# Attention and a ResMLP block on one core: another order of the first transposes, and one row turned by transfer

## The chip, the cores and the metric

One core of a Trainium2 chip runs the whole program. The metric is device microseconds of one execution, the median over runs. The engines named below: PE (TensorE, matrix products and transposes into PSUM), DVE (VectorE), ACT (ScalarE), POOL (GpSimd), SP (SyncE, which here only issues transfers). Transfers are issued from the queues of SP, POOL and ACT.

## The reference

Attention with 16 query heads and 4 key heads over 8 batches of 384 tokens, head size 64, and behind it a ResMLP block with width 1024 and 4096 hidden units:

```python
q, k, v: (8, 16, 384, 64), (8, 4, 384, 64), (8, 4, 384, 64)   # each k, v head serves 4 q heads
attn = softmax(q @ k.T / 8)                                    # per head
x = (attn @ v) as (8, 384, 1024)
a1 = alpha1 * x + beta1
tok = einsum('ts,bsd->btd', w_tok, a1)
u = x + lam * tok
a2 = alpha2 * u + beta2
out = u + lam * (relu(a2 @ w_ch1) @ w_ch2)
```

All inputs and the output are f32; the kernel computes its products in bf16.

## The kernel before

**Stages.** The kernel handles the batches in passes. Pass 0 and pass 1 multiply batches 0 and 1 by w_ch1 and w_ch2 (`main`). Passes 2, 3 and 4 take two batches each, (2, 3), (4, 5), (6, 7), and use a scheme of seven products instead of eight (`pair`). Such a scheme needs sums and differences of the blocks of its operands beforehand: `sums_a` builds them of the activations, `sum_w1` and `sum_w2` of the weights. The attention and the token mixing of the batches to come (`side`) are woven into the second product of the pass before: batch 0 stands alone at the start, batch 1 lies beside pass 0, batches 2 and 3 beside pass 1, 4 and 5 beside pass 2, 6 and 7 beside pass 3.

**The order is written out by hand.** Each engine executes its instructions in the order in which the program emits them. `main` and `pair` yield after every four matmuls or so; at each such place the program emits what `plan` holds for that place. For the second batch of a pair the places are those of its table plus 38 (`put_all(ps, 1, side(c + 1)[1], lambda u: u + 38)`).

**A side.** A batch's 16 heads are eight pairs p = 0 to 7, which are also eight rows of 128 columns of the 1024. `scores(i)` multiplies turned q and turned k (L279) into a PSUM tile of two banks, and ACT takes the exponential of 1024 columns at a time (L288). `av(p)` multiplies by v (L315), DVE divides (L320, L323) and scales (L328, L330). `tok_flip(p)` mixes the tokens (L340), adds (L347), scales to bf16 (L351), writes u out with a transfer from SP (`spill`, L243), and turns the row: a2 of row p must stand with its columns on the partitions before w_ch1 can use it. There are two ways to turn it:

- `a2_transpose(p)`, a transposing transfer from SP (L362), issued right behind the spill;
- `turn(p)`, three transposes on PE into a PSUM bank (L428) and one copy by ACT (L430), at a place of their own some steps later.

`by_pe(p)` chooses: for batch 1 row 7 is turned on PE; for batches 3, 5, 7 rows 5, 6, 7.

**Banks of a side beside a pair.** `three()` gives the three PSUM tiles sc0, sc1, sc2 out in turn, by the counter `pairs["turn"]`; while `pairs["held"]` is set, one of them belongs to the product and is passed over. Scores, av, tok and turn all take theirs from it. Beside pass 1 the three tiles come from a pool that rotates by itself.

**The hand-over.** For batches 4 to 7 `sums_a(0, 2)` stands at place 76, `sums_a(2, 1)` at 79 and `sums_a(3, 1)` at 81 of the pass before. Call (j, n) forms three sums (L587, L588, L589) from rows j to j + n - 1 and 4 + j to 4 + j + n - 1 of both batches; (0, 2) therefore reads rows 0, 1, 4 and 5. For batches 2 and 3 there are four calls at places 41, 42, 45 and 47, the second of which reads rows 1 and 5. In the next pass the first matmuls (X, L723, o = 1) read unmixed rows of the even batch; the ones behind them (Y, o = 7) read what L588 wrote, one row per matmul, rows j = 0 to 3 in order. Row 7 of batch 3 is written to the same buffer as its row 5 (two buffers, tag a2).

**The start.** Transfers bring k's heads 0 and 1 (SP, L150), the first two and the next two heads of q (ACT, L879), the other q groups, v and w_tok (POOL), and short rows of alpha, beta and lam (SP, L869). DVE and ACT cast k to bf16 twice side by side (`place_k`, L160). k is turned in bf16 on PE and copied by DVE (`k_transpose`, L255, L257); the first two pairs of q are turned in f32 straight from their staging area (`q_transpose`, L265) and copied by ACT (pair 0) or DVE (pair 1) (L267). `warmup(n)` emits n matmuls of 384 columns whose results nobody reads (L844): nine at the very start, three behind the first scores, one behind the fourth. `scale_rows` and `split` (L903, L911, L913) prepare the short rows on DVE; the first needs lam. The list `us` of `side(0)` is emitted front to back, and `load_k(1)` is emitted behind its fourth entry.

Of the kernel before, what the change touches and what calls it, by code (L numbers as in the profile page):

```python
# [12 lines left out]
def kernel(  # L13
# [40 lines left out]
    NP = Hq // 2  # L54
    D1 = D + 1
    NPL = 2
# [14 lines left out]
    threes, pairs = [], {}  # L71
# [23 lines left out]
    turn, a2_turn = [0], [0]  # L95
# [45 lines left out]
    def load_k(b, hs=(0, 2)):  # L141
        if b > 1:
            k_tile(b)
            for a in range(2):
                nc.gpsimd.dma_start(out=k2s[b][:, :, a], in_=by_head(k[b]))
            return
        for h in hs:
            ks[b, h // 2] = t = hTf[:, 7680 + 384 * h:8448 + 384 * h].bitcast(f32).rearrange(
                "p (h st d) -> p h st d", h=2, st=NST)
            nc.sync.dma_start(out=t, in_=by_head(k[b, h:h + 2]))  # L150
# [40 lines left out]
    def bank(shape, tag, name, dtype=f32):  # L191
        if tag == "mm":
            return mms.tile(shape, dtype, tag="mm", name=name, bufs=2)
        return psum.tile(shape, dtype, tag=tag, name=name, bufs=2 if tag == "sc" else 1)

    def three():
        if pairs:
            pairs["turn"] = (pairs["turn"] + 1 + (pairs["turn"] == 2 and pairs["held"])) % 3
            return pairs["sc%d" % pairs["turn"]].tile([P, 2, 4, P], f32, tag="sc", name="sc", bufs=1)
        return threes[0].tile([P, 2, 4, P], f32, tag="sc", name="sc", bufs=3)  # L200

    def one():
        return three()[:, 0]
# [25 lines left out]
    def side(b):  # L229
# [41 lines left out]
        def scores(i, later=False):  # L271
            sc = bank([P, 2, 4, P], "sc", "sc") if first else three()
            k = 4 * i
            while k < 4 * i + 4:
                n = min(4 * i + 4, k - k % NST + NST) - k
                p, sk, st = k // (NST * NST), k // NST % NST, k % NST
                for hh in range(2):
                    r = slice(hh * D, (hh + 1) * D)
                    nc.tensor.matmul(out=sc[:, hh, k % 4:k % 4 + n], lhsT=kT[r, 2 * p // G, BLK[hh][sk], :],  # L279
                                     rhs=qT[r, p, st:st + n, :], start=True, stop=True)  # L280
                k += n

            def exp():
                if first:
                    e = hTf[:, i % 6 * 1024:(i % 6 + 1) * 1024].rearrange("p (h k s) -> p h k s", h=2, k=4)
                else:
                    e = sb.tile([P, 2, 4, P], bf, tag="es", name="es", bufs=EB)
                nc.scalar.activation(out=e, in_=sc, func=EXP, scale=scale_qk)  # L288
                ess[i] = e
                exps[0] = 0 if first else 2  # L290

            if later:
                late.append(exp)
            else:
                exp()
# [40 lines left out]
        def tok(p):  # L336
            ps = bank([P, NST, P], "mm", "tok") if first else three()[:, 0, :NST]
            for tt in range(NST):
                for st in range(NST):
                    nc.tensor.matmul(out=ps[:, tt, :], lhsT=wtokT[:, st, tt * P:(tt + 1) * P],  # L340
                                     rhs=a1s[p][:, st, :], start=(st == 0),
                                     stop=(st == NST - 1 and not first))
                if first:
                    nc.tensor.matmul(out=ps[:, tt, :], lhsT=R[:, tt * P:(tt + 1) * P],
                                     rhs=H[:, cols(p)], start=False, stop=True)
            u = x_of(p)
            nc.vector.tensor_tensor(out=u, in0=ps, in1=u, op=ADD)  # L347
            if first:
                return
            a2s[p] = next_a2() if b > NPL + 1 else sb.tile([P, NST, P], bf, tag="a2", name="a2", bufs=2)  # L350
            nc.vector.tensor_tensor(out=a2s[p], in0=u, in1=bc(al2, p), op=MUL)  # L351
# [50 lines left out]
        def add(f, *a):  # L402
            us.append(lambda: f(*a))
# [12 lines left out]
        def flip(p):  # L416
            if not first:
                spill(p)
            if not by_pe(p):
                a2_transpose(p)  # L420

        def by_pe(p):
            return b % 2 and p >= (NP - 3 if b > NPL else NP - 1)

        def turn(p):
            ps = three()[:, 0].rearrange("p a b -> p (a b)").bitcast(bf)[:, :S].rearrange("p (a b) -> p a b", a=NST)
# [5 lines left out]
        if not first:  # L432


            turns = {}
            if b == 1:
                turns = {5: [(to_all, 3, 0, 0), (load_row_set, 1, 1, 0)], 7: [(to_all, 3, 1, 1), (load_row_set, 2, 0, 1)],
                         9: [(k_transpose, 0)], 12: [(to_all, 1, 0, 2)], 14: [(to_all, 1, 1, 0), (load_row_set, 2, 1, 0)],
                         17: [(scale_beta,)], 20: [(to_all, 2, 0, 1)], 22: [(to_all, 2, 1, 0)],
                         24: [(q_transpose, 0, 2, "av")], 28: [(k_transpose, 2)]}  # L440
                for i in range(3):
                    turns[32 + 4 * i] = [(q_transpose, 2 + 2 * i, 2, "av")]
            if (b - NPL) // 2 > 0:
                at = {}

                def put(k, *m):
                    at.setdefault(k, []).append(m)

                for j in range(6):
                    put((0, 6, 12, 21, 26, 31)[j], scores3, j, j in (2, 5))  # L450
                for p in range(NP):
                    put((4, 10, 14, 18, 24, 29, 33, 35)[p], av, p)
                    put((8, 15, 17, 22, 27, 32, 36, 38 if b % 2 else 39)[p], tok_flip, p)
                    if by_pe(p):
                        put((36, 39, 41)[p - NP + 3], turn, p)
                return turns, at
            return turns, {
                0: [(scores3, 0)], 4: [(av, 0)], 6: [(scores3, 1)], 8: [(tok_flip, 0)], 11: [(av, 1)],
                13: [(scores3, 2, True)], 15: [(av, 2)], 16: [(tok_flip, 1)], 18: [(tok_flip, 2)], 19: [(av, 3)],
                21: [(scores3, 3)], 23: [(tok_flip, 3)], 25: [(av, 4)], 27: [(scores3, 4)], 29: [(tok_flip, 4)],  # L460
                31: [(av, 5)], 33: [(scores3, 5, True)], 35: [(av, 6), (tok_flip, 5)], 37: [(av, 7)],
                38: [(tok_flip, 6)], 41: [(tok_flip, 7)],
                **{39 + 4 * i - i // 2 * 2: [(turn, p)] for i, p in enumerate((5, 6, 7)) if by_pe(p)}}
        add(k_transpose, 0, 1)
        add(q_transpose, 0, 1, "av", "ACT")
        add(place_k, 0, 0, (1,))
        add(q_transpose, 1, 1, "tp")
        lower, upper = range(NP // 2), range(NP // 2, NP)
        ut = a2_transpose
        at = {0: [(warmup, 3), (scale_rows, 0), (split, 0, 1, 0)], 1: [(k_transpose, 1, 1)],  # L470
              2: [(q_transpose, 2, 2, "av"), (split, 0, 1, 1)], 3: [(warmup, 1)],
              4: [(av, 0)], 5: [(spread, lower, "tp"), (a1, 0)], 6: [(av, 1), (k_transpose, 2, 2, "tp")],
              7: [(q_transpose, 4, 2, "av"), (a1, 1)], 8: [(av, 2)],
# [365 lines left out]
    with tc.manual_schedule(engines=order):  # L839

        def warmup(n):
            warm = bank([P, 512], "mm", "warm")
            for _ in range(n):
                nc.tensor.matmul(out=warm[:, :S], lhsT=wtokT[:, 0, :P], rhs=wtokT[:, 1, :],  # L844
                                 start=True, stop=True)

        nc.vector.memset(wtokT, 0.0)
        warmup(9)
        load_k(0, [0])

        rows_f = hTf[:32, 9216:10496].bitcast(f32)
# [107 lines left out]
        for i, f in enumerate(side(0)):  # L959
            f()  # L960
            if i == 3:
                load_k(1)
# [8 lines left out]
        def put(ps, phase, at, *m):  # L971
            plan.setdefault((ps, phase, at), []).append(m)
# [6 lines left out]
        def put_flips(ps, phase, b, places):  # L979
            for u, m in zip(places, ((flip_k, b), *((flip_q, b, i, 2) for i in range(0, NP, 2)))):  # L980
                put(ps, phase, u, *m)

        turns, at = side(1)
        put_all(0, 0, turns)
        put_all(0, 1, at)
        put_flips(0, 1, 2, (34, 36, 37, 42, 43))

        put(0, 1, 45, load_next, 3)
        put_all(1, 0, side(2)[1], lambda u: int(1.5 * u))
        put_flips(1, 0, 3, (53, 55, 57, 59, 61))  # L990
        put_all(1, 1, side(3)[1])
# [68 lines left out]
```

## Time and profile before

| | us |
|---|---|
| median of 3 runs | 740.01 (739.26 to 740.1) |
| the profiled execution, its own time | 739.53 |
| its span in the profile | 737.7 |
| PE busy in the span | 731.3 |
| DVE busy | 515.4 |
| ACT busy | 325.2 |
| mean granted PE clock | 0.999 of full |

The span runs from the first instruction of the program to the end of the last; the execution's own time has 1.83 us around it. All durations of single instructions below come from that one execution. A line of the timeline gives start, length, engine, line of the code, operation and tiles; several instructions of one kind in a row are merged (x3), and the length is then that of the group. Matmul records overlap, since the next one starts before the last one has drained; what a matmul costs PE is the distance from start to start.

What the transfers that turn rows look like, and who turned rows on PE (all instructions that write or read the tile `ops`):

```profile
L362 SPq DMA_TRANSPOSE ops<-obuf x26: 1238/1288/2234, 326.9 to 570.0; - x26
L362 SPq DMA_TRANSPOSE ops<-a x20: 1240/1296/3387, 87.0 to 225.0; - x20
L430 ACT COPY ops<-sc x10: 479/480/480, 129.0 to 585.4; 128x384 bf16<-128x384 bf16 x10
DMA to landing us min/median/max: 2.4/5.0/9.8
```

The first two lines are issues (ns: shortest, median, longest), and the last is the time from issue to landing for those of them that the view could match.

### The profile page before, as it was taken

How to read it: one execution, taken by the hardware profiler on the slowest of the kernel's cores; microseconds unless marked ns; L12 is line 12 of the kernel's file. 1: busy time of each engine (PE TensorE's matmuls, PEld its weight loads, DVE VectorE, ACT ScalarE, POOL GpSimd, SP SyncE). 2: the span in 40 equal slices, each digit the busy share in tenths (PEclk: the TensorE clock that was granted, in tenths of full speed). 3: DMA queues.
4: the chain of work that ended last, by engine and by line, in shares of the span. 5: the costliest groups of instructions: out<-in, count | busy, mean ns of one | idle time of the engine just before them, and what ended most of it. 6: DMA issues, size and time to landing. Idle time of an engine off the chain costs nothing.

```text
span 737.7 us, 14512 instructions
## 1 busy us (share of the span) xinstructions
PE 731.3 (99%) x5769; PEld 418.9 (57%) x5769; DVE 515.4 (70%) x993; ACT 325.2 (44%) x469; POOL 164.0 (22%) x211
## 2 busy tenths in 40 slices
PE   8999999999999999999999999999999999999998
PEld 5866555566555566655555566555555566654444
DVE  7773366457587889749777987847968988762354
ACT  7632431455332566653334366664343266660000
POOL 9434221420000232211012244020002222000011
PEclk9999999999999999999999999999999999999999
DMA  9999999999999999999979999998989999937965
GB/s 187 194 201 200 207 216 174 176 187 208 217 271 257 179 221 212 260 269 201 296 186 219 181 145 192 207 246 199 269 242 152 223 136 143 173 115 262 288 189 103
DMA packets 218017, 151.32 MB, mean 205 GB/s; under 512 B 88660, under 2 KB 197060, under 8 KB 217948
## 3 DMA queue, kind: packets, MB, share of 16 engines
q0 software_dynamic: 120304, 64.60, 67.0%
q1 hardware_dynamic: 96956, 85.33, 42.7%
q8 instruction: 45, 0.74, 0.4%
q10 hardware_dynamic: 688, 0.46, 0.2%
q14 instruction: 24, 0.20, 0.1%
HBM read 154.84 MB, written 38.27 MB: 262 GB/s over the span
## 4 chain that ended last, share of the span: by engine, by line
PE 93%; DVE 3%; DMA 3%; SPq 1%; issue 0%; ACT 0%; DVEq 0%
PE C L789 30%; PE X L723 17%; PE h L532 10%; PE ch L570 9%; PE Y L723 8%; PE sc L279 4%; PE Z L723 4%; PE sc L315 4%; PE sc L340 3%; DMA ops<-a 2%; PE h L223 1%; DMA hT<-in_moe_lam_dram 1%; PE tok L340 1%; SPq L176 0%; PE av L315 0%; DVE xr L323 0%
## 5 line engine op out<-in xcount | busy, mean ns | idle before, releaser
L288 ACT ACTIVATE es<-sc 128x1024 bf16<-128x1024 f32 x126 | 121.4, 1023 | 155.9 <-PE sc L279 144.8
L789 PE MATMUL C<-w,arena 128*128 128x512 bf16 (+2 forms) x744 | 168.3, 372 | 0.0
L789 PEld LDWEIGHTS <-arena 128*128 128x128 bf16 x1040 | 94.8, 98 | 100.5 <-issue 5.1
L728 ACT ACTIVATE hT<-X,bias 128x384 f32<-128x384 f32 x144 | 83.7, 582 | 61.8 <-PE X L723 54.8
L723 PEld LDWEIGHTS <-w 128*128 128x128 bf16 x768 | 75.1, 98 | 50.1 <-issue 0.2
L517 POOL DMA_DIRECT2D out_dram<-hT x33 | 28.8, 871 | 283.5 <-DVE hT L688 106.1
L570 PE MATMUL ch<-arena,hT 128*128 128x512 bf16 x384 | 90.8, 379 | 0.0
L185 POOL DMA_DIRECT2D w<-in_moe_w_ch_dram x68 | 62.8, 965 | 98.2 <-PE X L723 34.2
L532 PE MATMUL h<-ops,w 128*128 128x384 bf16 (+1 forms) x480 | 83.3, 327 | 0.3
L723 PEld LDWEIGHTS <-pad 128*128 128x128 bf16 x576 | 56.4, 98 | 37.2
L723 PE MATMUL X<-ops,w 128*128 128x384 bf16 x384 | 70.2, 326 | 0.0
L723 PE MATMUL X<-ops,pad 128*128 128x384 bf16 x384 | 70.2, 326 | 0.0
L789 PE MATMUL C<-pad,arena 128*128 128x512 bf16 (+2 forms) x296 | 70.2, 373 | 0.0
L532 PEld LDWEIGHTS <-w 128*128 128x128 bf16 x480 | 45.4, 98 | 29.8 <-issue 2.1
L570 PEld LDWEIGHTS <-hT 128*128 128x128 bf16 x384 | 34.7, 98 | 36.8 <-issue 2.5
L347 DVE TENSOR_TENSOR xr<-sc,xr 128x384 f32<-128x384 f32 x56 | 31.0, 553 | 24.3 <-PE sc L340 24.3
L315 PEld LDWEIGHTS <-es 128*128 128x128 bf16 x1008 | 38.3, 97 | 12.4
L340 PEld LDWEIGHTS <-wtokT 128*128 128x128 bf16 x576 | 37.5, 98 | 11.8 <-DVE a L330 0.8
L279 PE MATMUL sc<-qT,kT 64*128 64x384 bf16 (+2 forms) x576 | 41.8, 271 | 0.7 <-DVE xr L323 0.3
L320 DVE RECIPROCAL rinv<-sc 128x6 f32<-128x6 f32 x56 | 10.8, 192 | 44.3 <-PE sc L315 44.1
L315 PE MATMUL sc<-v,es 128*128 128x65 bf16 x1008 | 39.9, 193 | 0.0
L723 PE MATMUL Z<-ops,w 128*128 128x384 bf16 x192 | 39.0, 326 | 0.0
(138 smaller groups left out, 910.3 us busy)
## 6 DMA issues: line engine op xcount, KB each, us to landing
w<-in_moe_w_ch_dram POOLq DMA_DIRECT2D x68, 512.0 KB, 10.7
w<-w2s SPq DMA_DIRECT2D x60, 512.0 KB, 4.6
pad<-w2s SPq DMA_DIRECT2D x24, 512.0 KB, 7.2
out_dram<-xr SPq DMA_DIRECT2D x56, 192.0 KB, 6.1
out_dram<-hT POOLq DMA_DIRECT2D x33, 256.0 KB, 6.0
arena<-in_moe_w_ch_dram POOLq DMA_DIRECT2D x16, 512.0 KB, 20.0
w2s<-arena SPq DMA_DIRECT2D x28, 256.0 KB, 4.9
q_raw<-in_q_dram POOLq DMA_DIRECT2D x28, 192.0 KB, 10.6
```

The lines of the kernel that those rows point to most:

```text
L185: nc.gpsimd.dma_start(out=w1[:, w1_slots[c]], in_=w1src[:, :, c * CW * P:(c + 1) * CW * P])
L279: nc.tensor.matmul(out=sc[:, hh, k % 4:k % 4 + n], lhsT=kT[r, 2 * p // G, BLK[hh][sk], :], rhs=qT[r, p, st:st + n, :], start=True, stop=True)
L288: nc.scalar.activation(out=e, in_=sc, func=EXP, scale=scale_qk)
L315: nc.tensor.matmul(out=av[:, hh, sq, :], lhsT=ess[k // 4][:, m % 2, k % 4, :], rhs=vb[:, sk, hk, :], start=(sk == 0), stop=(sk == NST - 1))
L340: nc.tensor.matmul(out=ps[:, tt, :], lhsT=wtokT[:, st, tt * P:(tt + 1) * P], rhs=a1s[p][:, st, :], start=(st == 0), stop=(st == NST - 1 an ...
L347: nc.vector.tensor_tensor(out=u, in0=ps, in1=u, op=ADD)
L517: nc.gpsimd.dma_start(out=at, in_=o, accum_op=ADD)
L532: nc.tensor.matmul(out=ps[:, :n], lhsT=w1[:, w1_slots[c], dt, j * P:(j + 1) * P], rhs=a2T[:, dt, :n], start=(dt == 0), stop=(dt == NDT - 1))
L570: nc.tensor.matmul(out=ps, lhsT=hT[:, nt, ms * P:(ms + 1) * P], rhs=w2[:, row(nt)[0], row(nt)[1], cs], start=(i == 0), stop=(i == NNT - 1))
L723: nc.tensor.matmul(out=ps, lhsT=tb[g, o][:, dt, e * P:(e + 1) * P], rhs=opb(LEFT1[o])[:, dt], start=(o in (1, 2, 7) and dt == 0), stop=(dt ...
L728: nc.scalar.activation(out=snap[o, e], in_=ps, func=IDENT, bias=hi if o == 5 else lo)
L789: nc.tensor.matmul(out=x, lhsT=hid[:, t, LEFT2[o], ms * P:(ms + 1) * P], rhs=rhs[:, t % 4 * 512 + c0:t % 4 * 512 + c1], start=((not last o ...
```

## The change

Two things are changed.

**At the start** the first pair of q is turned in front of k instead of behind it, and the second pair of q is turned behind the first scores (as the first entry of that place) instead of in front of them. The idle matmuls in front are six instead of nine, and behind the first scores two instead of three.

**For the odd batches of the pairs** (3, 5 and 7) `by_pe` now takes rows 6 and 7 only. Row 5 goes the way of rows 0 to 4: a transposing transfer behind its spill. Where its `turn` stood beside a pair (place 36), the new `next_bank` moves the counter of the three tiles on by one and nothing else, so that every later user gets the tile that it had. Batch 3 has no such step.

```diff
+    def next_bank():
+        pairs["turn"] = (pairs["turn"] + 1 + (pairs["turn"] == 2 and pairs["held"])) % 3
+
     def three():
         if pairs:
-            pairs["turn"] = (pairs["turn"] + 1 + (pairs["turn"] == 2 and pairs["held"])) % 3
+            next_bank()
...
         def by_pe(p):
-            return b % 2 and p >= (NP - 3 if b > NPL else NP - 1)
+            return b % 2 and p >= (NP - 2 if b > NPL else NP - 1)
...
                     if by_pe(p):
                         put((36, 39, 41)[p - NP + 3], turn, p)
+                    elif b % 2 and p == NP - 3:
+                        put(36, next_bank)
...
+        add(q_transpose, 0, 1, "av", "ACT")
         add(k_transpose, 0, 1)
-        add(q_transpose, 0, 1, "av", "ACT")
         add(place_k, 0, 0, (1,))
-        add(q_transpose, 1, 1, "tp")
...
-        at = {0: [(warmup, 3), (scale_rows, 0), (split, 0, 1, 0)], 1: [(k_transpose, 1, 1)],
+        at = {0: [(q_transpose, 1, 1, "tp"), (warmup, 2), (scale_rows, 0), (split, 0, 1, 0)], 1: [(k_transpose, 1, 1)],
...
-        warmup(9)
+        warmup(6)
```

## The prediction

> **What bounds the kernel now.** I read the page first: busy shares, then the chain that ended last.
>
> ```profile
> span 737.7 us, 14512 instructions
> PE 731.3 (99%) x5769; PEld 418.9 (57%) x5769; DVE 515.4 (70%) x993; ACT 325.2 (44%) x469; POOL 164.0 (22%) x211
> PE 93%; DVE 3%; DMA 3%; SPq 1%; issue 0%; ACT 0%; DVEq 0%
> ```
>
> TensorE is busy 99% of the span and is 93% of the chain, so time taken off TensorE is time gained, unless another wait takes its place. The DVE and DMA shares sit in a few places. Both parts of the change touch one: the first 16 us, and the hand-over from the second matrix product of a pair to the next pair.
>
> The chain in order of time (start, length), over the first 45 us:
>
> ```profile
> 2.16 5.32 DMA hT<-in_moe_lam_dram
> ...
> 7.58 0.29 DVE hT L903
> 7.89 0.54 DVE hT L911
> 8.46 0.48 DVE hT L913
> 8.93 0.27 DVE kT L257
> 9.20 0.47 DVE qT L267
> ...
> 15.46 0.27 DVE wtokT L372
> ```
>
> Until 15.7 us the end is set neither by TensorE nor by the exponentials on ACT. The small transfer of lam lands at 7.48; DVE waits for it at L903 and then works in its order, with gaps of under 0.06 us, until the last copy of w_tok at 15.7. From there the chain is TensorE.
>
> The timeline shows the first scores, and what their order costs:
>
> ```profile
> 1.52 3.06 PE L844 MATMUL warm<-wtokT 128*128 128x384 bf16 x9 [1.52 <-DVE wtokT L847]
> 3.97 0.54 DVE L160 CAST k<-hT 128x192 bf16<-128x192 f32 x1 [0.34 <-DMA hT<-in_k_dram]
> 4.57 0.50 PE L255 MATMUL tp<-ident,k 128*128 128x128 bf16 x3
> 4.86 1.42 PE L265 MATMUL tp<-hT,arena 128*128 128x128 f32 x6
> 6.28 0.39 PE L279 MATMUL sc<-qT,kT 64*128 64x384 bf16 x4
> 6.60 0.66 PE L844 MATMUL warm<-wtokT 128*128 128x384 bf16 x3
> ```
>
> Nine idle matmuls start every 0.32 us, later ones of the same shape every 0.17: the clock records rise from half to full at 6.01.
>
> **The change, start.** k's cast ends at 4.51. The first q transfer, issued at 0.73, should land near 4.27: the second was issued at 1.25 and landed at 4.78, 3.53 later. Six idle matmuls end at 1.52 + 6 x 0.32 = 3.44, so TensorE waits 0.85 us and turns the first pair of q from 4.3 to 4.96 (3 x 0.213, the spacing of the f32 ones at 5.07 and 5.29). Then k: three at 0.107, done near 5.5, its copy on DVE (0.36) near 5.87. First scores: 5.9 instead of 6.28, 0.38 earlier. The second pair of q (0.3 to 0.6) comes behind them. ACT's first exponential gains some 0.3; the second, whose scores now wait behind q's transposes, 0.2.
>
> What is this worth at 15.7? DVE stood idle 0.70 us before L903 and the lam transfer is issued as before, second on SP behind alpha; nothing ahead of it moves. So the DVE chain starts at 7.58 again. The second pair's copy of q is then ready near 6.7 and done by 7.3: hidden in that same idle time, which is its cover; without the cover each 0.1 us of it would be 0.1 of the end. Value taken: **0**. Bounds: -0.38 (all that the scores gain) to +0.7 (clock, below). Moving load_k(1) in the program leaves it on SP behind the casts of k's other head, at 6.5 before and 6.4 after.
>
> **The change, row 5 of batches 3, 5 and 7.** Removed on TensorE: three transposes per batch (L428). Their records are 0.33 long, but what counts is start to start:
>
> ```profile
> 579.33 0.33 PE L428 MATMUL sc<-ident,obuf 128*128 128x128 bf16 x3
> 579.50 0.67 PE L340 MATMUL sc<-a,wtokT 128*128 128x128 bf16 x9
> ```
>
> 0.17 us, at full clock and with no wait: 3 x 0.17 = **-0.51 us**. ACT's three copies of 0.48 (L430) go too; ACT is idle 2.47 before them, worth nothing. The bank's turn is skipped by a counter: no cost. In batch 3 the rotation of the three banks does shift by one, but each following user gets a bank freed earlier, so nothing.
>
> Added on SP: one transposing transfer per batch, behind the spill of row 5. Issues take 1.24 to 3.39 us. In batches 5 and 7 SP has nothing else until the next spill at 582.18 (L243, issue 575.56): free. In batch 3 it pushes copies of w2 by about 1 us; they have no reader on the chain.
>
> What counts is when the row lands, for a new wait: sums_a(0, 2) on DVE (L587 to L589) reads rows 0, 1, 4, 5. Behind it DVE has the sums of rows 2 and 3, sum_w1 and L826, and the new pair's first Y product reads row 3's difference:
>
> ```profile
> 575.56 8.82 SPq L243 DMA_DIRECT2D out_dram<-xr  x3
> ...
> 584.33 0.55 DVE L587 TENSOR_TENSOR ops<-ops 128x768 bf16<-128x768 bf16 x1
> ...
> 588.62 1.46 PE L723 MATMUL X<-ops,w 128*128 128x384 bf16 x8
> 589.57 0.36 DVE L588 TENSOR_TENSOR ops<-ops 128x384 bf16<-128x384 bf16 x1
> 589.92 0.81 PE L723 MATMUL Y<-ops,w 128*128 128x384 bf16 x4
> ```
>
> DVE is busy 12.62 of the 13 us from 575 to 588, so a wait at 584.33 goes through unabsorbed. Row 3's difference ends at 589.93; the fourth Y matmul reads it at 589.92 + 3 x 0.163 = 590.41. Less 0.04 for the signal the slack is 0.44, and 0.27 once TensorE arrives 0.17 sooner.
>
> When does it land? Not by the page's median of 4.6 us, but by neighbours in the same stage, from the trace's semaphores: issued at 390.43, 396.66, 563.75, 569.98 they took 9.83, 6.75, 10.08, 8.47. Better, each lands shortly behind its spill: 0.4 to 0.6 us (five pairs), 1.9 (one), or 2.6 to 2.8 where POOL's weight loads are moving (two). Row 5's spills landed at 408.32 and 584.15, and DVE needs the row at 411.02 and 584.33.
> - Batch 5: 408.7 to 411.1. At most 0.13 late, inside the slack: 0.
> - Batch 7: 584.6 to 586.95. Late by 0.4 to 2.7 with the signal, less 0.27: a stall of 0.1 to 2.4. POOL's queue moves some 390 packets/us from 584 on, which speaks for the upper half, but the first two microseconds after the spill may be shared evenly; I take the middle, **+1.25**.
> - Batch 3: lands 2.8 to 6.0 after 232.5 by its five neighbours, so by 238.5. Its buffer is wanted by row 7 at 237.40 and its sum at 238.80; DVE has 1.58 idle before L577 at 242.32: 0.
>
> The Trainium skill ("VectorE: DVE Perf Modes", The three transpose paths) gives 1309 ns for a 128x128 turn by transfer against 390 ns on TensorE, and advises TensorE where PSUM will do. By that price, as an estimate, three blocks take 3.9 us, the row would be there at 580, and the sum would be -0.51. The trace differs: no transfer of this kind in that stage took under 6.7 once the weight loads had begun.
>
> Sum: 0 - 0.51 + 1.25 = **+0.74**: span 737.7 to 738.4. The profiled execution took 739.53, 1.83 outside its span, and is 0.48 under the median of the runs shown, so 740.01 + 0.74 = **740.75**. This kernel's runs can tell about 0.2%, 1.5 us.
>
> **Rivals.**
> *Row 5 is late in both pairs (slower).* One mechanism: its packets queue with the weight loads that POOL issues at 402.02 and 575.34, just before. It decides from the moment the row lands over 0.27 us behind DVE's arrival. For it: between the two pairs the same spill differs by 2.5 us against DVE's arrival (2.70 ahead of it, 0.18 ahead), so batch 5 can fall where batch 7 is. Against: it did not in this execution. At 2.2 per pair: 4.4 - 0.51 = +3.9, 743.9; with batch 7 alone at its upper end +1.7 to +1.9, 741.8.
> *Row 5 in time everywhere.* Stalls nought: -0.51, 739.5. For it: five pairs of eight land 0.6 or less behind their spill. Against: batch 7's spill itself lands 0.18 before the need.
> *The clock rises a step later.* The records give full clock at 6.01 and half again at 736.47, 730.45 = 214 x 3.413 apart, so decisions seem to fall on a grid of 3.41. TensorE was busy through the stretch 2.60 to 6.01 and only from 1.52 in the one before, which did not raise it. After the change 2.60 to 6.01 holds holes of 0.85 and 0.4. If that is too little, half clock lasts to 9.4: first scores 5.9 to 6.4, q 7.1, two idle ones 7.7, second scores 8.25, k 8.6, third scores 9.1, q(2,3) done 9.8, and its copy on DVE at 9.8 where it was 9.13: **+0.7**, alone with the -0.51 740.2, with the forecast's stall 741.4. For it: the one stretch that raised it was busy throughout; against: 63% busy may do.
> The Trainium skill ("TensorE: Matmul & The Clock Gate", Part 1 and Part 4) says that the gate watches a free-running window of 3413 ns and that transposes do not count as busy in the same way; by this the stretch would be only some 30% busy and this rival would be the forecast. The grid agrees with the trace; that transposes count less no run here shows.
> *The start does gain.* If lam lands sooner in other executions, the exponentials lead: -0.38 - 0.51 = -0.9, 739.1. Against: 0.70 idle before L903.
>
> **Chances.** Forecast (late in batch 7 only, by the middle, stall 0.5 to 2) 0.37; late at the upper end or in both 0.26; in time 0.15; clock 0.14; start gains 0.08. The likeliest one's own range is 740.0 to 741.5. The whole range reaches from the last, 739.1, to between one and two full stalls, 743.0: 739.0 to 743.0. Slower by over 0.2% (741.5 up): the late case, part of the clock's (with a stall on top) and of the forecast's upper edge, 0.36. Faster (under 738.5): no case reaches it, only something unseen, 0.08. The rest 0.56.
>
> **What would show it.** First scores at 5.9 and L903 still at 7.5 to 7.6; the clock's rise at 6.0 or 9.4; no L428 for row 5; a DVE wait on `ops<-obuf` at L587 near 411 and 584, a gap on TensorE before Y near 416 and 590. Wrong, if L903 starts earlier, if the row lands before DVE is there, or if the gap at Y is over 2.5.

## The result, and the profile after

The changed kernel takes 742.84 us (median of 6 runs, 741.22 to 743.26) where the kernel before took 739.51 on the same chip (6 runs, 739.16 to 740.1): a ratio of 1.0041, 95% interval 1.0028 to 1.0054, some 3.3 us slower. The profiled execution took 743.26, its span is 741.5. First the page: span, busy time, and the shares of the chain that ended last.

```profile
span 741.5 us, 14432 instructions
PE 727.5 (98%) x5697; PEld 418.0 (56%) x5756; DVE 514.0 (69%) x993; ACT 324.2 (44%) x466; POOL 163.9 (22%) x211
PE 84%; DVE 7%; DMA 5%; issue 3%; POOL 1%; ACT 0%; DVEq 0%; POOLq 0%
```

No engine has more work than before. What grew is waiting: DVE and DMA have 12% of the chain where they had 6%. (Some matmul records are missing in this trace; that is part of the "issue" share.)

To find where, the start of every weight load of TensorE was compared with the same one of before. The difference along the profiled execution, and the steps in it:

| place, time in before | after minus before, us | what is there |
|---|---|---|
| 15.8 | +1.40 | the start |
| 108 and 132 | 1.09 | 0.31 made good, no changed code |
| 234 | 0.92 | row 5 of batch 3 no longer turned on TensorE |
| 408, 581 | 0.2 earlier, then 0.2 later again | row 5 of batches 5 and 7, given back within 2.3 us |
| 453 | +1.0 | DVE waits for a weight load that landed 2.26 later |
| 590 | +1.12 | the hand-over behind batch 7 |
| last matmul | 3.04 | |
| end of the span | 3.76 | +0.72 behind the last matmul |

**The start.** The chain of waits of the first 17 us (start, length):

```profile
0.73 3.57 DMA arena<-in_q_dram
...
4.43 0.89 PE tp L268 x3
...
6.08 0.60 PE sc L282 x4
6.68 0.83 PE tp L268 x3
7.51 0.64 PE warm L848 x2
8.15 0.54 PE sc L282 x4
...
16.87 0.28 DVE wtokT L375
```

Before, the chain ran through the transfer of lam to DVE's first addition on the short rows, and the second w_tok copy ended it at 15.73; now it runs through TensorE itself, and the same copy ends at 17.15. The timeline shows why TensorE is in it:

```profile
4.43 0.88 PE L268 MATMUL tp<-hT,arena 128*128 128x128 f32 x3 [0.81 <-DMA arena<-in_q_dram]
...
6.08 0.61 PE L282 MATMUL sc<-qT,kT 64*128 64x384 bf16 x4 [0.45 <-ACT k L160]
...
7.55 0.56 DVE L270 CAST qT<-tp 128x384 bf16<-128x384 f32 x1 [1.36 <-PE tp L268]
...
8.03 0.27 DVE L907 TENSOR_TENSOR hT<-hT 32x128 f32<-32x128 f32 x1
...
10.46 0.56 DVE L270 COPY qT<-tp 128x768 bf16<-128x768 bf16 x1 [0.58 <-PE tp L268]
```

Three f32 transposes take 0.88 instead of the 0.52 that they take at full clock. The clock records give the rise at 10.55 instead of 6.01. The copy of q's second pair on DVE starts at 7.55 and pushes the first addition on the short rows (L907, L903 of before) from 7.58 to 8.03, and the next copy of q waits for TensorE until 10.46 (9.13 before).

**Row 5.** All instructions on the tile `ops`:

```profile
L365 SPq DMA_TRANSPOSE ops<-obuf x28: 1239/1310/2185, 327.8 to 578.1; - x28
...
L433 ACT COPY ops<-sc x7: 479/480/480, 130.3 to 587.3; 128x384 bf16<-128x384 bf16 x7
```

Two more transfers beside the pairs, three fewer copies by ACT. Row 5 landed at 411.84 in batch 5 and at 587.69 in batch 7. The timeline at the second hand-over:

```profile
587.78 0.56 DVE L591 TENSOR_TENSOR ops<-ops 128x768 bf16<-128x768 bf16 x1 [1.47 <-DMA ops<-obuf]
...
591.84 0.65 PE L727 MATMUL Y<-ops,w 128*128 128x384 bf16 x3
...
593.04 0.36 DVE L592 TENSOR_TENSOR ops<-ops 128x384 bf16<-128x384 bf16 x1
...
593.45 0.32 PE L727 MATMUL Y<-ops,w 128*128 128x384 bf16 x1 [0.95 <-DVE ops L592]
```

The last bracket of a line is the idle time ahead of it and what ended it. DVE stood 1.47 us in front of the first sum, until row 5 had landed; everything behind it on DVE moved, and TensorE waited 0.95 in front of the fourth Y matmul, whose row L592 had just written. At 411.94 there was no wait.

**The given-back transposes.** Why two of the three removed turns bring nothing is seen just behind row 5's old place in batch 7. First the change, then the same second place in the kernel before, where nothing was waited for:

```profile
581.16 0.56 PEld L343 LDWEIGHTS <-wtokT 128*128 128x128 bf16 x9 [0.26 <-DVE a L333]
...
583.65 0.50 PEld L343 LDWEIGHTS <-wtokT 128*128 128x128 bf16 x9 [0.52 <-DVE a L333]
```

```profile
581.51 0.71 PEld L340 LDWEIGHTS <-wtokT 128*128 128x128 bf16 x9
```

TensorE now arrives earlier at the token mixing of rows 6 and 7 and waits for DVE, which scales these rows (L333) and has no idle time there.

**The end.** From the last matmul to the end of the span it is 4.27 us (737.22 to 741.49), before 3.55 (734.18 to 737.73). The last output transfer, issued by ACT, takes longer to land. The DMA view from its issue to its landing, after and then before (packets, MB, share of 16 engines):

```profile
q1 hardware_dynamic: 144, 0.20, 25.0%
q10 hardware_dynamic: 144, 0.07, 10.1%
q14 instruction: 1, 0.01, 1.2%
...
out_dram<-ends ACTq DMA_DIRECT2D x1, 64.0 KB, 2.2
```

```profile
q1 hardware_dynamic: 144, 0.20, 34.4%
q10 hardware_dynamic: 144, 0.07, 13.8%
...
out_dram<-ends ACTq DMA_DIRECT2D x1, 64.0 KB
```

The same packets on both queues, and ACT's transfer lands 2.18 after its issue instead of 1.59; in between moves one packet of kind instruction: 1.2% of 16 engines over 2.18 us is 0.42 us of one engine. In the kernel before such a packet moves too, but at 737.7, when all has landed.

### The profile page after: what moved, and what is told of

It is laid out like the page before. It is cut to its first block, busy times and chain, and to the rows that moved or that the text cites. A ratio compares the mean times of both kernels' runs of the same rounds, so it can differ in the third digit from the quotient of the medians.

```text
span 741.5 us, 14432 instructions
## 1 busy us (share of the span) xinstructions
PE 727.5 (98%) x5697; PEld 418.0 (56%) x5756; DVE 514.0 (69%) x993; ACT 324.2 (44%) x466; POOL 163.9 (22%) x211
## 4 chain that ended last, share of the span: by engine, by line
PE 84%; DVE 7%; DMA 5%; issue 3%; POOL 1%; ACT 0%; DVEq 0%; POOLq 0%
PE C L793 25%; PE X L727 14%; PE h L536 10%; PE ch L574 10%; PE Y L727 7%; PE sc L282 5%; PE Z L727 4%; PE sc L318 3%; PE sc L343 3%; DMA w<-in_moe_w_ch_dram 2%; DMA ops<-obuf 1%; DMA ops<-a 1%; PE h L226 1%; DVE xr L326 1%; DVE xr L350 1%
## 5 line engine op out<-in xcount | busy, mean ns | idle before, releaser
L793 PE MATMUL C<-w,arena 128*128 128x512 bf16 (+2 forms) x711 | 163.7, 372 | 1.6 <-issue 0.3
L574 PE MATMUL ch<-arena,hT 128*128 128x512 bf16 x366 | 87.6, 379 | 0.9 <-issue 0.3
L727 PE MATMUL Y<-ops,w 128*128 128x384 bf16 x192 | 39.2, 326 | 1.8 <-DVE ops L592 1.0
```

Source lines behind the costliest of these rows:

```text
L574: nc.tensor.matmul(out=ps, lhsT=hT[:, nt, ms * P:(ms + 1) * P], rhs=w2[:, row(nt)[0], row(nt)[1], cs], start=(i == 0), stop=(i == NNT - 1))
L727: nc.tensor.matmul(out=ps, lhsT=tb[g, o][:, dt, e * P:(e + 1) * P], rhs=opb(LEFT1[o])[:, dt], start=(o in (1, 2, 7) and dt == 0), stop=(dt ...
L793: nc.tensor.matmul(out=x, lhsT=hid[:, t, LEFT2[o], ms * P:(ms + 1) * P], rhs=rhs[:, t % 4 * 512 + c0:t % 4 * 512 + c1], start=((not last o ...
```

## The experiments

The theory after the result: three costs that add. The start lets the clock rise a step later; row 5 is waited for at the hand-over; the rest is either chance or something that neither names. Rivals: it is all row 5; it is all the start; the traffic of the transfers, not the wait for them, costs. Each kernel was timed beside the kernel before on the same chip; what follows are medians in us, with the ratio and its interval. The text in front of each diff says which kernel it starts from.

**1 to 3: one part alone.** *The start alone*, from the change: row 5 of all batches turned on TensorE.

```diff
-            return b % 2 and p >= (NP - 2 if b > NPL else NP - 1)
+            return b % 2 and p >= (NP - 3 if b > NPL else NP - 1)
```

> The start alone is changed (order of q and k, six and two idle matmuls); row 5 is turned on PE as before. My theory (the cost is shared: a later rise of the clock at the start, and row 5 landing late in the last pair): slower than before by 0.4 to 1.8 us, with the clock's rise one or more steps of 3.41 us later than the first possible one (in the trace of the change it was 10.55, the first matmul of w_ch1 1.40 late), and no DVE wait on a transposing transfer at the last hand-over. Rival 'all of it is row 5': within 0.4 us of before. Rival 'all of it is the start', the wait for weights near 453 us included: +2.4 to +3.3. That wait (1.0 us on PE) is put to neither part beforehand; the trace shows whether it is there.

*Row 5 alone*, from the change: the order, and the nine and three idle matmuls, of before.

```diff
+        add(k_transpose, 0, 1)
         add(q_transpose, 0, 1, "av", "ACT")
-        add(k_transpose, 0, 1)
         add(place_k, 0, 0, (1,))
+        add(q_transpose, 1, 1, "tp")
...
-        at = {0: [(q_transpose, 1, 1, "tp"), (warmup, 2), (scale_rows, 0), (split, 0, 1, 0)], 1: [(k_transpose, 1, 1)],
+        at = {0: [(warmup, 3), (scale_rows, 0), (split, 0, 1, 0)], 1: [(k_transpose, 1, 1)],
...
-        warmup(6)
+        warmup(9)
```

> Row 5 of batches 3, 5 and 7 by transfer, with the start of before. My theory: the clock rises by 8.4 us at the latest, the first matmul of w_ch1 is within 0.3 us of before; -0.17 in batch 3, about 0 in batch 5, a DVE wait of 1 to 2.5 us at the sums of rows 0, 1, 4, 5 in the last pair and 0.7 to 2 us lost on PE there: +0.3 to +1.7 in all. Rival 'all of it is the start': -0.5 to 0. Rival 'all of it is row 5' (its packets push later transfers too): +2.4 to +3.3, with the wait near 453 us.

*The order alone*, from the start alone: nine and three idle matmuls again, so that only the order of the transposes is new.

```diff
-        at = {0: [(q_transpose, 1, 1, "tp"), (warmup, 2), (scale_rows, 0), (split, 0, 1, 0)], 1: [(k_transpose, 1, 1)],
+        at = {0: [(q_transpose, 1, 1, "tp"), (warmup, 3), (scale_rows, 0), (split, 0, 1, 0)], 1: [(k_transpose, 1, 1)],
...
-        warmup(6)
+        warmup(9)
```

> The new order of q and k with nine and three idle matmuls, as before the change; row 5 on PE. My theory (the clock needs a stretch of PE without holes): the hole in front of the first q transposes shrinks from 0.8 to under 0.1 us, one of some 0.4 stays in front of the first scores; if holes of 0.4 in 3.4 do no harm the clock rises by 8.4 at the latest and the time is within 0.4 us of before, since DVE waits for lam at about 7.5 either way; if such a hole already does harm it is +0.4 to +1.8 like the start alone. Rival 'the order itself costs' (q's second pair behind the scores delays DVE, whatever the clock): +0.5 or more with the clock's rise where it was. Rival 'the order gains': -0.3.

Measured, against 739.5: the start alone 740.79 (1.0015, 1.0007 to 1.0024), row 5 alone 740.91 (1.0019, 1.0007 to 1.003), the order alone 739.84 (1.0000, 0.9992 to 1.0009). So the two parts cost some 1.3 and 1.4, and the order as such nothing: with nine idle matmuls the first scores came at 5.56, 0.72 earlier, lam was waited for until 7.30, and at 15.8 the difference was -0.02. The gain of the scores ends in the wait for lam.

In the profiled execution of row 5 alone (740.91, its median) the forecast wait is missing. Row 5 landed at 411.44 and at 584.63, 0.13 and 0.15 before the sum that reads it, and neither hand-over cost anything. Its time went elsewhere: 0.85 to a wait at 133 for the transfer of a row of batch 1, ahead of any changed code, and 0.94 more than before to the stretch behind the last matmul. The two lines:

```profile
133.33 1.95 PE L537 MATMUL h<-ops,w 128*128 128x384 bf16 x11 [0.85 <-DMA ops<-a]
...
584.78 0.55 DVE L592 TENSOR_TENSOR ops<-ops 128x768 bf16<-128x768 bf16 x1
```

So the wait is a matter of the execution: the +1.4 has the forecast size, but this profile does not show the forecast cause.

**4: row 5 in batches 3 and 5 only**, from row 5 alone.

```diff
-            return b % 2 and p >= (NP - 2 if b > NPL else NP - 1)
+            return b % 2 and p >= (NP - (2 if b < B - 1 else 3) if b > NPL else NP - 1)
```

> Start of before; row 5 by transfer in batches 3 and 5 only, on PE in batch 7. My theory (only the last pair pays): -0.17 in batch 3, 0 to -0.17 in batch 5, nothing at the last hand-over: -0.4 to 0 against before, and 0.7 to 2 us under the kernel with row 5 by transfer in all three. Rival 'batch 5 is as late as batch 7': +0.3 to +1.7. Rival 'the start pays all': the same as row 5 in all three within 0.3 us.

Measured: 741.18 against 739.5 (1.0022, 1.0012 to 1.0032). That is no less than with batch 7, a miss of the theory that batch 5 is always in time. The timeline shows batch 5's hand-over in this execution:

```profile
414.70 0.56 DVE L592 TENSOR_TENSOR ops<-ops 128x768 bf16<-128x768 bf16 x1 [1.33 <-DMA ops<-obuf]
```

Row 5 landed at 414.68, and the shift of TensorE grew by 0.98 there. So either hand-over can be the late one. The rival "batch 5 is as late as batch 7" fits the number, though not by this wait alone. (This execution also lost 2.8 us between 150 and 170, ahead of any changed code.)

**5: the change again.** The same kernel, for a second profile.

> The change once more, whole, beside its parts on one chip. If the parts add up (the start alone +1.2, row 5 alone +1.4): 741.9 to 742.4, with the clock's rise after 8.4 us, the first matmul of w_ch1 1.2 to 1.5 late, and a stall of 0.5 to 2 us at the last hand-over. If the two parts hurt each other (the wait near 453 us comes from both together): 742.8 or more, and that wait is seen again.

Measured: 743.18 against 739.78 (1.0041, 1.0028 to 1.0054). The profiled execution (742.01): +1.29 at 15.8, clock up at 8.19; +0.44 at 417 and +0.64 at 590, the two hand-overs; nothing at 453. The +1.0 at 453 was thus of one execution, the start and the hand-overs are of both. Behind the last matmul again 4.29. The median, 3.4 above the kernel before, lies over the 741.9 to 742.4 of parts that add up and in the range of parts that hurt each other, but the sign named for that, the wait at 453, is missing. The intervals of the parts are wide enough for a plain sum; whether they only add up stays open.

**6: fewer idle matmuls alone**, from before: the old order with six and two.

```diff
-        at = {0: [(warmup, 3), (scale_rows, 0), (split, 0, 1, 0)], 1: [(k_transpose, 1, 1)],
+        at = {0: [(warmup, 2), (scale_rows, 0), (split, 0, 1, 0)], 1: [(k_transpose, 1, 1)],
...
-        warmup(9)
+        warmup(6)
```

> The order of before (k first), but six and two idle matmuls in place of nine and three. My theory (PE without work for a good part of a stretch of 3.41 us leaves the clock at half; the order is harmless): a hole of about 1.1 us in front of k's transposes, the clock's rise in many executions later than in before, 0.3 to 1.5 us slower, like the start of the change (+1.2). Rival 'the order with six does it': within 0.3 us of before. A rise that still comes at 6.0 to 7 in the one trace would not settle it, since the steps lie anywhere; then the times of the runs decide.

Measured: 740.02 against 739.78 (1.0001, 0.9993 to 1.001). The profiled execution had the clock up at 10.86 and +1.36 at 15.8, and took 740.75, the longest of eleven. So in this one execution the late rise costs as much in the old order, but the median, 0.24 up, is the rival's case ("the order with six does it", within 0.3). What the other executions did differently stays open: they have no record of when the clock rose.

**7: the short rows behind the copy of k's second head**, from the order alone.

```diff
-        at = {0: [(q_transpose, 1, 1, "tp"), (warmup, 3), (scale_rows, 0), (split, 0, 1, 0)], 1: [(k_transpose, 1, 1)],
+        at = {0: [(q_transpose, 1, 1, "tp"), (warmup, 3)], 1: [(k_transpose, 1, 1), (scale_rows, 0), (split, 0, 1, 0)],
```

> New order with nine and three idle matmuls; besides, scale_rows and split stand behind the copy of k's second head on DVE instead of in front of it. My theory (the start is bound by lam's landing and DVE's order behind it): DVE does the copy of k (0.27 start to start) in the idle time before lam, so its chain at 15.7 us is about 0.25 earlier than in before, and the first matmul of w_ch1 0.1 to 0.3 earlier; 739.2 in the mean. Rival 'PE or the exponentials bind the start': no change at 15.7 us against the new order alone, or the whole 0.6 that the exponentials start earlier.

Measured: 740.10 against 739.78 (1.0004, 0.9995 to 1.0013), no gain. The first addition moved to 8.29, behind that copy, and at 15.8 the difference was +0.85, somewhat more than the 0.71 by which the addition is late. So here a later L903 (L907 in this kernel) makes a later end of the start. It is not the only thing that can: in the profile of the passenger (10 below) the addition starts at 7.31, earlier than in the kernel before, and the end is still 0.44 late. There the clock rose at 7.21, and the chain runs through TensorE and ACT's exponentials instead of lam.

**8: the sum that reads row 5 done later**, from row 5 alone: rows 0 and 1 of the hand-over are summed by two calls, row 1 with row 5 at place 79.

```diff
-            for j, u in ((0, 76), (2, 79), (3, 81)):
-                put(ps, 1, u, sums_a, j, 1 if j else 2)
+            for j, u in ((0, 76), (2, 79), (1, 79), (3, 81)):
+                put(ps, 1, u, sums_a, j)
```

> Start of before; row 5 by transfer in all three batches, but the sums of rows 1 and 5 are split from those of rows 0 and 4 and done behind those of rows 2 and 6, some 3.5 us later on DVE. My theory (the loss is DVE's wait for the row, in its order, at the first sums): no DVE wait on the transfer at either hand-over, the split costs DVE 0.4 us of which 0.1 to 0.2 reaches PE: -0.3 to +0.1 against before, 1 to 1.5 under row 5 by transfer alone. Rival 'the transfer's traffic delays the others': the same +1.4 as row 5 by transfer alone. Rival 'the missing transposes on PE are worth nothing': 0 to +0.4.

Measured: 740.74 against 739.78 (1.0014, 1.0005 to 1.0023). In the profiled execution row 5 of batch 7 landed at 586.30, as late as ever, and nobody waited (the sum that reads it is the one at 587.43):

```profile
584.37 0.35 DVE L592 TENSOR_TENSOR ops<-ops 128x384 bf16<-128x384 bf16 x1
...
587.43 0.35 DVE L592 TENSOR_TENSOR ops<-ops 128x384 bf16<-128x384 bf16 x1
...
589.98 0.81 PE L728 MATMUL Y<-ops,w 128*128 128x384 bf16 x4
```

No bracket on the sums, none on Y. The wait is gone and the median is still 1.0 up: half a miss, and a sign that row 5 costs something besides the wait. How much of the +1.4 of row 5 alone the wait is, the medians do not settle, since the two intervals overlap.

**9: row 5 in batch 3 only**, from row 5 alone. **10: row 5 as a passenger**, from before: turned on TensorE, and sent through the transfer as well, to a place that nobody reads.

```diff
-            return b % 2 and p >= (NP - 2 if b > NPL else NP - 1)
+            return b % 2 and p >= (NP - (2 if b == NPL + 1 else 3) if b > NPL else NP - 1)
```

> Start as before, row 5 turned by transfer in batch 3 alone; batches 5 and 7 turn it on TensorE again. Theory (what row 5 costs is in the hand-overs from pair to pair, where DVE or TensorE meets the late row): nothing is lost, three transposes are gained at 234: median -0.2 against before, within -0.4 to +0.1, and the single runs no wider than before's. Rival (the new transfer pushes the copies of w2 behind it on SP, and these push what follows): +0.5 to +1.5, as the kernel with batches 3 and 5 showed (+1.4), with a shift that appears between 240 and 330 us.

```diff
+    sink = const.tile([P, 2, P], bf, tag="sink", name="sink")
...
             if not by_pe(p):
                 a2_transpose(p)
+            elif b > NPL and p == NP - 3:
+                src = a2s[p].rearrange("p a d -> p (a d)")
+                nc.sync.dma_start_transpose(out=sink, in_=src[:, :2 * P])
+                nc.sync.dma_start_transpose(out=obuf.bitcast(bf)[:, 5 * S:5 * S + P], in_=src[:, 2 * P:])
```

> The kernel before with its start and all its turns on TensorE, and in batches 3, 5 and 7 row 5 is also sent through the transposing transfer, behind the same spill, to a place that nobody reads (as two issues, of two blocks and one block). Theory (the cost is the wait for the row): nobody waits for it, so -0.2 to +0.3 against before, no gap on TensorE at 416 and 590. Rival (the cost is the traffic, or the queue of SP behind the extra issue: weights, spills and rows behind it land later): +0.6 to +1.5, as wide as with row 5 by transfer, with a gap on TensorE or DVE that ends with another transfer's landing.

Measured, against 739.46: batch 3 only 740.14 (1.0007, 0.9998 to 1.0016), the passenger 739.47 (0.9998, 0.999 to 1.0007). The passenger's timeline at batch 7:

```profile
576.45 1.88 SPq L424 DMA_TRANSPOSE sink<-obuf  x1
578.38 1.22 SPq L425 DMA_TRANSPOSE obuf<-obuf  x1
...
584.57 0.55 DVE L592 TENSOR_TENSOR ops<-ops 128x768 bf16<-128x768 bf16 x1
...
590.17 0.81 PE L728 MATMUL Y<-ops,w 128*128 128x384 bf16 x4
...
593.62 0.69 DVE L632 TENSOR_TENSOR pad<-w 128x1024 bf16<-128x1024 bf16 x1 [1.99 <-issue]
...
595.24 1.47 PE L728 MATMUL X<-ops,w 128*128 128x384 bf16 x8 [0.35 <-DVE ops L747]
```

Its two transfers landed at 587.51 and 588.09, some 3 us after DVE's sum had begun, and nobody waited for them. But in front of 593.62 DVE stood 1.99 us, and TensorE lost 0.53 behind it. The bracket names no releaser; what landed just before, at 593.54, is a weight load issued by POOL (tile w, which this sum reads), 17.06 after its issue (11.4 to 16.1 in the thirteen other profiles). That is the sign which the rival named. The median does not show it: this execution (740.22) is the second longest of eleven, and the ratio's interval leaves the traffic and the extra issue at most some 0.5 us. On the median they cost nothing that can be measured; that a single execution can pay for them is not excluded. Batch 3 alone was forecast at -0.2 and came out 0.7 up by the medians, with an interval that just reaches nothing; its profile shows TensorE where it should be (+0.12 at the last matmul, 0.16 gained at 234), and no shift between 240 and 330 as the rival had it, but 4.21 us behind the last matmul instead of 3.55.

**11 and 12: which hole at the start.** Both from the order alone (nine and three): six and three idle matmuls, then nine and two.

```diff
-        warmup(9)
+        warmup(6)
```

> The change's order of the transposes, six idle matmuls in front instead of nine, three behind the first scores as before, row 5 on TensorE. Theory (the loss at the start comes from the hole in front of the first transposes, between the last idle matmul and the landing of q: the stretch of the clock's grid that holds it is not enough to raise the clock, and while it is at half the second pair's copy on DVE runs past lam): as the whole start did, +0.8 to +1.4 against before, and in the profile, if the clock rises behind 7.5, the short rows' first addition on DVE at 7.8 to 8.2. Rival (the hole behind the first scores does it, the third idle matmul there covers it): 0 to +0.3.

```diff
-        at = {0: [(q_transpose, 1, 1, "tp"), (warmup, 3), (scale_rows, 0), (split, 0, 1, 0)], 1: [(k_transpose, 1, 1)],
+        at = {0: [(q_transpose, 1, 1, "tp"), (warmup, 2), (scale_rows, 0), (split, 0, 1, 0)], 1: [(k_transpose, 1, 1)],
```

> The change's order of the transposes, nine idle matmuls in front, two behind the first scores instead of three, row 5 on TensorE. Theory (the hole in front matters): 0, within -0.3 to +0.4, the clock's rise before 7.5. Rival (the hole behind the first scores does it): +0.8 to +1.4, with the rise at 8 to 11.

Measured, against 739.73: six and three 740.66 (1.0011, 1.0003 to 1.002), nine and two 739.88 (0.9999, 0.9988 to 1.0009). With the order of the change, the hole in front of the first transposes is the one that counts. The timelines, six and three first, then nine and two:

```profile
4.36 0.87 PE L268 MATMUL tp<-hT,arena 128*128 128x128 f32 x3 [0.74 <-DMA arena<-in_q_dram]
...
7.48 0.56 DVE L270 CAST qT<-tp 128x384 bf16<-128x384 f32 x1 [1.37 <-PE tp L268]
7.96 0.62 DVE L907 TENSOR_TENSOR hT<-hT 32x128 f32<-32x128 f32 x1
```

```profile
4.48 0.52 PE L268 MATMUL tp<-hT,arena 128*128 128x128 f32 x3
...
6.53 0.56 DVE L270 CAST qT<-tp 128x384 bf16<-128x384 f32 x1 [0.53 <-PE tp L268]
...
7.30 0.28 DVE L907 TENSOR_TENSOR hT<-hT 32x128 f32<-32x128 f32 x1 [0.21 <-DMA hT<-in_moe_lam_dram]
```

With six, TensorE waits for q and works at half speed, and the short rows wait for the copy of q. With nine the copy is over and the short rows wait for lam.

**All profiles side by side.** One profiled execution each: when the clock rose, how late the last w_tok transposes were at 15.8, and the time from the last matmul to the end of the span.

| kernel | idle in front | rows 5 by transfer | clock up at | at 15.8 | behind the last matmul |
|---|---|---|---|---|---|
| before | 9 | 0 | 6.01 | 0 | 3.55 |
| order alone | 9 | 0 | 4.53 | -0.02 | 3.54 |
| order, nine and two | 9 | 0 | 4.37 | -0.01 | 3.52 |
| short rows later | 9 | 0 | 5.55 | +0.85 | 3.54 |
| passenger | 9 | 0 | 7.21 | +0.44 | 3.47 |
| row 5, batch 3 | 9 | 1 | 6.85 | +0.30 | 4.21 |
| row 5, batches 3 and 5 | 9 | 2 | 4.22 | -0.26 | 4.07 |
| row 5 alone | 9 | 3 | 4.50 | -0.01 | 4.49 |
| row 5, sum later | 9 | 3 | 7.37 | +0.51 | 4.46 |
| start alone | 6 | 0 | 10.18 | +1.32 | 3.52 |
| fewer idle alone | 6 | 0 | 10.86 | +1.36 | 3.54 |
| order, six and three | 6 | 0 | 10.53 | +1.72 | 3.55 |
| the change | 6 | 3 | 10.55 | +1.40 | 4.27 |
| the change again | 6 | 3 | 8.19 | +1.29 | 4.29 |

Two columns fall apart cleanly. With nine idle matmuls in front the clock rose between 4.22 and 7.37, with six between 8.19 and 10.86. Within the nine, too, the three latest rises (6.85 to 7.37) go with +0.30 to +0.51 at 15.8. And every kernel in which row 5 is really turned by transfer ends 4.07 to 4.49 behind its last matmul, every other one 3.47 to 3.55. That last term, 0.5 to 0.9 us, is what the kernels with the later sum and with batch 3 alone had left over: 0.91 of 1.0, and 0.66 - 0.16 = 0.50 of 0.7.

In the four profiles with all three transfers the last output transfer took 2.18 to 2.40 us to land, and in all four a packet of kind instruction moved beside it; in the others it took 1.58 to 1.60, without one. With one or two transfers it landed on time, and the time is lost in SP's last waits (1.75 and 1.63 us from that landing to the end, instead of 1.11). The edit changes no instruction of the last stage. What it changes there is by how many instructions the program is shorter on TensorE and longer on SP. That the fetch of instructions thereby falls into the last transfer is what the profiles suggest; no kernel was run that moves this alone, so it is not shown. The passenger is longer on SP by six issues and not shorter on TensorE, and does not have the loss; nor do the kernels that only leave out three or four idle matmuls.

## Why the prediction was right or wrong

The time forecast was 2.1 below the first median. That the median lies within the range, 0.16 under its top, is luck: the top stood for one to two full stalls of row 5, and not for a start 1.3 late and a later end. The outcome held likeliest (within 0.2%, 0.56) did not come; slower, at 0.36, did. The sum, 0 - 0.51 + 1.25, was wrong in two of its terms and left one out; that they fell on the same side made it too low.

**The start, "Value taken: 0": wrong, +1.3.** The two readings that it rested on hold: without the loss of the clock the first scores come earlier (5.56) and the end does not move, since lam leads (the order alone). The failing step is the choice between value and rival: the clock's later rise was priced as a rival at +0.7 with a chance of 0.14, and it is what happens, in all five profiles with six idle matmuls. Its price was off as well, 0.7 against 1.3 to 1.4 in the two profiles of the change. The second and third scores were forecast at 8.25 and 9.1 and came at 8.09 and 9.06; but full clock was assumed from 9.4 on, as if the grid lay where it lay in the kernel before; it came at 10.55, so the six transposes of q's next pairs, begun at 9.60, lasted until 10.4 instead of 9.8 and the copy behind them moved from 9.13 to 10.46. The cover named for the second pair's copy (DVE idle before L903) was gone too, as the prediction priced it: the copy, forecast over by 7.3, kept DVE until 8.03 and took L903 with it.

The argument for the rival was there: the one stretch known to raise the clock was busy throughout. Against it stood "63% busy may do", a guess. By the records each of the five profiles with six idle matmuls has a stretch of 62 to 68% ahead of the rise that did not do; in the profile of the change 3.72 to 7.13, which holds the hole, was 66% busy (50% with transposes).

**"-0.51" for nine transposes: -0.17.** Only batch 3's turn is gained (0.16 to 0.17 at 234 in every profile where it was removed). Beside the pairs TensorE comes 0.2 earlier to the token mixing of the next rows and waits for DVE. The prediction had the reading at hand, "DVE is busy 12.62 of the 13 us", and used it for the wait, not for the gain: time taken off an engine is only kept if the next engine that it meets has slack.

**Batch 3 and batch 5 "0", batch 7 "+1.25": right in mechanism, and nearly in size in one profile.** Batch 7 cost 1.12 and 0.64 in the two profiles of the change, batch 5 cost 0 and 0.44, and 0.98 in the kernel without batch 7: it can be late, as the rival "late in both pairs" had it, but not by the 2.2 each that it was priced at. In the profile of row 5 alone both cost 0, which is the rival "in time everywhere". The forecast took one of several outcomes between which executions differ. Landing was forecast at 584.6 to 586.95 in before's time and came at 587.69, which less the shift of that stage (1.92) is 585.77; so reckoned, the four profiles with batch 7's transfer have 584.16 to 586.24, against a need at 584.33. That it is the wait and not the traffic, the passenger's median speaks for, with the 0.53 of its one profile as an open end.

**Not named by any case: +0.7 behind the last matmul.** The prediction followed the change to its last wait and took the end as given.

Together, from the profile of the change: 1.40 - 0.17 + 1.12 + 0.72 is 3.07, and with the steps of -0.31 and +1.0 it is the 3.76 of the span. The +1.0 is of that execution. The -0.31 is not: ten of the twelve other profiles also step back 0.21 to 0.28 at 132, so it lies in the one profile of the kernel before with which all are compared. By medians, the start 1.3 and row 5 1.4 make 2.7 of the 3.3 to 3.4 measured, inside the intervals of all three. What is shown by runs is the start (nine idle matmuls take its loss away) and that row 5 costs; how its cost divides between the wait and the end, and what makes the end later, is not. No kernel here is faster than the one before; the best of them, the passenger and the order alone, equal it.

## What to carry to other kernels

Idle matmuls that keep the clock coming are not spare time: before taking some away, ask of each hole that this opens whether the stretch that raises the clock is still busy, and follow the half-speed operations to the next engine. A gain on a busy engine counts only up to the next engine with no slack, and a transfer that replaces work must be held against its reader in each place where it is read, not against a median. When a small edit moves the time by more than its parts, look also at what lies behind the last matmul.

## What was not expected of the hardware

The clock rises and falls on a grid: in the change 10.55 and 741.00 are 730.45 us apart, in the other profiles 727.04, 730.45, 733.87 or 737.28, which is 213 to 216 times 3.413. Where the grid lies differs from run to run. If one bound on the busy share of a stretch decides, the stretches between its points tell where it lies (by the matmul records, whose ends are modelled). The windows of the kernel with fewer idle matmuls alone, and of row 5 in batches 3 and 5 (length, then the busy time of TensorE):

```profile
4.03:7.45 3.42, 2.88 (x15) 1.51 (x15) 2.25 (x6) 1.43 (x4) 3.42 (x6) 1.00 1.63 185
```

```profile
0.81:4.22 3.41, 2.70 (x9) 1.19 (x9) 2.56 (x14) 1.50 (x2) 2.86 (x6) 1.00 0.66 181
```

The first, 84% busy, did not raise the clock; the second, 79% busy, did. The first is mostly transposes (only 32% of the stretch are other matmuls), the second holds none. On the other side a stretch of the change's second profile, 4.78 to 8.19, raised the clock with 87% busy (40% of the stretch with other matmuls), while 71% of idle matmuls alone (row 5 with the later sum, 0.54 to 3.96) did not. All fourteen profiles fit a bound between 71 and 79% if a transpose counts as 0.66 to 0.9 of another matmul; counting it fully or not at all does not fit. The Trainium skill ("TensorE: Matmul & The Clock Gate", Part 4) says of the transpose mode that "it doesn't count as PE-busy the same way"; the traces agree so far, but by this reckoning it does count for more than half.

The other surprise is the end: one packet of kind instruction, 0.43 to 0.65 us of one DMA engine, beside a last transfer of 64 KB that in these four profiles lands 0.6 to 0.8 us later. That the packet is the reason is not shown.
